# The first loads of an attention and gated-unit kernel: one hardware transfer instead of four, the rest cast on GpSimd's queue, and the first grams ahead of the transposes

## The chip, the cores and the metric

The kernel runs on one core of a Trainium2 chip. The metric is the device time of one execution in microseconds (us). "Before" and "after" are the kernel without and with the change. The medians of before in the four groups of experiments lie within 0.2 us (172.70 to 172.91), its single executions within 1.4 us (172.28 to 173.63), so a difference of 0.3 us between medians is near the limit of what can be told. Some changed kernels spread over 2 us; it is said where it matters. Ratios use runs in the fast state alone. Two runs, one of e8 and one of the repeat of e4, were in the slow state and are left out.

## The reference

Attention with pooled queries, then a gated unit with a causal convolution over time:

```python
q_pool = q.reshape(B, H, S // 2, 2, D).mean(axis=3)         # B = H = 8, S = 1152, D = 64
attn   = softmax(q_pool @ k.T / sqrt(D))
x      = (attn @ v), heads side by side                      # 8 x 576 x 512
gate   = sigmoid(causal convolution of x, 5 taps per channel)
out    = (gate * (x @ w_val)) @ w_out                        # float32
```

q, k and v are float32, 18.9 MB each. The kernel replaces the softmax by its first-order form (the scores are small; a flag computed at the end sends other data to an exact version). It therefore needs column sums of k and v and the "gram" matrices k-transposed times v, and uses q only after transposing it.

## The kernel before

Work goes by "slots" of four heads, sixteen slots in all. A slot has three loads (q, k, v), which GpSimd issues and which turn float32 into bfloat16 on the way. The first pair of heads was special: uncast loads through the hardware queues of SyncE and ScalarE, cast afterwards on VectorE and ScalarE.

```python
def load_slot(m, lo=0):                       # GpSimd's queue, with cast; lo: first head loaded
    ...
    nc.gpsimd.dma_start(out=qns[m][:, lo:], in_=q[...])
    for c, src in ((1, k), (0, v)):
        nc.gpsimd.dma_start(out=kvs[m][:, c, lo:], in_=src[...])

for h in range(2):
    nc.sync.dma_start(out=q0[:, h], in_=q[0, h]...)              # 2 x 0.29 MB, float32
nc.scalar.dma_start(out=kv0[:, 1], in_=k[0, 0:2]...)             # 0.59 MB
nc.sync.dma_start(out=kv0[:, 0], in_=v[0, 0:2]...)               # 0.59 MB
load_slot(0, 2)                               # second pair of slot 0: GpSimd, cast
...
warm(12)                                      # matmuls on zeros, for the clock
pool_q(0); transposes(0)
... wval, wout, load_slot(2), load_slot(3)
nc.vector.tensor_copy(out=kvs[0][:, 1, 0:2], in_=kv0[:, 1])      # cast of k
nc.scalar.copy(out=kvs[0][:, 0, 0:2], in_=kv0[:, 0])             # cast of v
pool_q(1)
# slot 0: sums(pair 0), grams(0), transposes(1), setup_conv, sums(pair 1), rows, grams(1), ...
# slot m: sums, rows, grams, ... ; load_slot(m + 4); output stores wait until all loads are issued
```

Of the kernel before, what the change touches and what calls it, by code (L numbers as in the profile page):

```python
# [7 lines left out]
FP32 = mybir.dt.float32  # L8
# [46 lines left out]
def first_order(ctx, tc, q, k, v, moe_w_val, moe_conv_w, moe_w_out, out, flag):  # L55
    nc = tc.nc
    B, H, S, D = q.shape
# [3 lines left out]
    NT = S // 128  # L61
# [4 lines left out]
    U = 6  # L66
    QP = Sq // U
# [9 lines left out]
    kv_pool = ctx.enter_context(tc.tile_pool(name="kvp", bufs=NKV))  # L77
    q_pool = ctx.enter_context(tc.tile_pool(name="qp", bufs=NKV))
# [12 lines left out]

    kvs, qns = {}, {}

    def load_slot(m, lo=0):
        b, h0 = divmod(4 * m, H)
        kvs[m] = kv_pool.tile([128, 2, 4, NT * D], BF16, name="kv", tag="kv")
        qns[m] = q_pool.tile([QP, 4, 2 * U * D], BF16, name="qn", tag="qn")
        nc.gpsimd.dma_start(out=qns[m][:, lo:], in_=q[b, h0 + lo:h0 + 4].rearrange("h (p s) d -> p h (s d)", p=QP))  # L98
        for c, src in ((1, k), (0, v)):
            nc.gpsimd.dma_start(out=kvs[m][:, c, lo:],  # L100
                                in_=src[b, h0 + lo:h0 + 4].rearrange("h (p t) d -> p h (t d)", p=128))


    q0 = q_pool.tile([QP, 2, 2 * U * D], FP32, name="q0", tag="qn")
    kv0 = kv_pool.tile([128, 2, 2, NT * D], FP32, name="kv0", tag="kv")
    for h in range(2):
        nc.sync.dma_start(out=q0[:, h], in_=q[0, h].rearrange("(p s) d -> p (s d)", p=QP))
    nc.scalar.dma_start(out=kv0[:, 1], in_=k[0, 0:2].rearrange("h (p t) d -> p h (t d)", p=128))
    nc.sync.dma_start(out=kv0[:, 0], in_=v[0, 0:2].rearrange("h (p t) d -> p h (t d)", p=128))

    wval_sb = consts.tile([128, NFT, Dm], BF16, name="wval_sb")
    wout_sb = consts.tile([128, NFT, Dm], BF16, name="wout_sb")
    convw_nat = consts.tile([KK, Dm], FP32, name="convw_nat")
    nc.sync.dma_start(out=convw_nat, in_=moe_conv_w)
    load_slot(0, 2)

    ident = consts.tile([128, 128], BF16, name="ident")
    nc.vector.memset(ident, 0.0)
# [17 lines left out]
    for i in range(2):  # L136
        for h in range(2):
            p = slice(64 * h + 32 * i, 64 * h + 32 * i + 32)
# [17 lines left out]
    for i in range(NX):  # L156
        t = xp_pool.tile([128, PAD + Sq], BF16, name=f"x{i}", tag=f"x{i}")
# [25 lines left out]
    for i in range(2):  # L183
        t = mq_pool.tile([128, 2, MQ], BF16, name=f"mq{i}", tag=f"mq{i}")
# [6 lines left out]

    def pool_q(n):
        m, i = divmod(n, 2)
        src = qns[m][:, 2 * i:2 * i + 2] if n else q0
        qv = src.rearrange("p h (u e d) -> p h u e d", u=U, e=2)
        qps[n] = work.tile([QP, U, 2, D], BF16, name="qp", tag="qp", bufs=3)
        nc.vector.tensor_tensor(out=qps[n].rearrange("p u h d -> p h u d"),  # L197
                                in0=qv[:, :, :, 0, :], in1=qv[:, :, :, 1, :], op=ALU.add)

    def transposes(n, at=None):  # L200
        m, i = divmod(n, 2)
        qp = qps.pop(n)
        qt_ps = (ps_t if at is None else ps_b).tile([128, Sq], BF16, name="qt_ps", tag="ts" if at is None else f"b{at}")
        qtv = qt_ps.rearrange("c (u p) -> c u p", u=U)
        for u in range(U):
            nc.tensor.transpose(out=qtv[:, u, :], in_=qp[:, u].rearrange("p h d -> p (h d)"),  # L206
                                identity=ident[0:QP, 0:QP])
        nc.scalar.copy(out=mq2[m % 2][:, i, 2 * D:].rearrange("c (p u) -> c p u", u=U),  # L208
                       in_=qt_ps.rearrange("c (u p) -> c p u", u=U))
# [15 lines left out]
    def grams(n):  # L225
        m, i = divmod(n, 2)
        kvv = kvs[m].rearrange("p c h (t d) -> p c h t d", t=NT)
        if i == 0:
            gs[m] = ps_g.tile([128, 512], FP32, name="g", tag="g")
        for t in range(NT):  # L230
            for h in range(2):
                nc.tensor.matmul(out=gs[m][64 * h:64 * h + 64, 128 * i:128 * i + 128].rearrange("p (c d) -> p c d", c=2),  # L232
                                 lhsT=kvv[:, 1, 2 * i + h, t, :], rhs=kvv[:, :, 2 * i + h, t, :],
                                 start=(i == 0 and t == 0), stop=(t == NT - 1), skip_group_check=True)
# [185 lines left out]
                             skip_group_check=True)  # L420

    warm(12)
    pool_q(0)
    transposes(0)
    nc.gpsimd.dma_start(out=wval_sb, in_=moe_w_val.rearrange("(ft p) n -> p ft n", p=128))
    nc.gpsimd.dma_start(out=wout_sb, in_=moe_w_out.rearrange("(ft p) n -> p ft n", p=128))
    load_slot(2)
    load_slot(3)
    nc.vector.tensor_copy(out=kvs[0][:, 1, 0:2], in_=kv0[:, 1])
    nc.scalar.copy(out=kvs[0][:, 0, 0:2], in_=kv0[:, 0])  # L430
    pool_q(1)
    for m in range(NSLOT):
        a, b = 2 * m, 2 * m + 1
        pb = b - 2
        odd = m % 2
        if m == 0:
            sums(m, (0,))
            grams(a)
            transposes(b, 1)
            setup_conv()  # L440
            sums(m, (1,))
            rows(m)
            grams(b)
        else:
            sums(m)
            rows(m)
            grams(a)
            grams(b)
        rank1(m)
        g = gs.pop(m)  # L450
        mevac(m, g)
        if not odd:

            bt = m // 2 - 1
            y, e = divmod(bt, 2)
            moe = bt >= 0
            if moe:
                pool_q(a + 2)
                tap(pb, 1)
            if moe:  # L460
                gval(bt, 2, val(bt, 2, 0))
            xhat(a, 1)
            xhat(b, 2)
            xevac(a)
            if moe:
                gate(pb)
            xevac(b)
            if m:
                norms(m - 1, g)
            squares_k(m, g)  # L470
            if moe:
                transposes(a + 2)
                gval(bt, 3, val(bt, 3, 0))
                stat(m - 1, g)
                pool_q(b + 2)
            else:
                pool_q(a + 2)
                transposes(a + 2)
            squares(m)
            conv(a, 1)  # L480
            conv(b, 2)
            tap(a, 0)
            if not moe:
                pool_q(b + 2)
            tap(a, 1)
            tap(a, 2)
            if moe:
                ops = big("ops", 0)
                outs(y, 512 * e, 4, ops, [0])
            transposes(b + 2)  # L490
            if moe:
                outs(y, 512 * e, 4, ops, [1])
                oevac(y, 512 * e, 4, ops)
            gate(a)
        else:

            bt = (m - 1) // 2
            y, e = divmod(bt - 1, 2)
            moe = bt > 0
            for i in range(3):  # L500
                tap(pb, i)
            if moe:
                if e:
                    ops = big("ops", 0)
                    outs(y, 1024, 1, ops, [0])
                    oevac(y, 1024, 1, ops)
                else:
                    ops = big("ops", 0)
                    outs(y, 0, 4, ops, [2])
            xhat(a, 1)  # L510
            xhat(b, 2)
            xevac(a)
            xevac(b)
            if moe and e:
                norms(m - 1, g)
            squares_k(m, g)
            if m + 1 < NSLOT:
                pool_q(a + 2)
                pool_q(b + 2)
            if moe:  # L520
                if e:
                    ops = big("ops", 0)
                    outs(y, 512, 4, ops, [2])
                    conv(a, 1)
                outs(y, 512 * e, 4, ops, [3])
                oevac(y, 512 * e, 4, ops, 2)
                if not e:
                    conv(a, 1, 1)
            else:
                conv(a, 1)  # L530
            if m + 1 == NSLOT:
                squares(m)
            conv(b, 2, 3 if m + 1 == NSLOT else 1)
            if not (moe and e):
                norms(m - 1, g)
            tap(a, 0)
            stat(m - 1, g)
            if m + 1 < NSLOT:
                transposes(a + 2)
            gate(pb)  # L540
            tap(a, 1)
            if e or not moe:
                tap(a, 2)
            if m + 1 == NSLOT:
                gate(b)
            else:
                tap(b, 0)
            gval(bt, 0, val(bt, 0, 1))
            if m < NSLOT - 1:
                transposes(b + 2)  # L550
            gate(a)
            gval(bt, 1, val(bt, 1, 0))
            if m + 1 < NSLOT:
                squares(m)
            if m == 1:
                warm(5, 1)
        if m + NKV < NSLOT:
            load_slot(m + NKV)
        else:
            while held:  # L560
                store(*held.pop(0), nc.gpsimd)
# [202 lines left out]
```

## Time and profile before

| | before |
|---|---|
| median | 172.77 us (172.68 to 173.12) |
| span in the profile | 170.5 us |
| matmul engine (PE) busy | 149.1 us, 87% |
| VectorE (DVE), ScalarE (ACT), GpSimd (POOL) busy | 125.1, 112.3, 44.1 us |
| HBM | 58.73 MB read, 9.44 MB written |

A busy share says how much an engine worked, not that the end waited for it. The prediction shows the rows that matter, those of the DMA rate and of the landings.

### The profile page before, as it was taken

The page shows a single profiled execution, that of the slowest core. Times are in us where ns is not written, and L with a number is a line of the kernel's source. Part 1 is how long each engine was busy: PE and PEld are TensorE (multiplying, and loading weights), DVE is VectorE, ACT ScalarE, POOL GpSimd, SP SyncE. Part 2 cuts the span into 40 slices and gives each one's busy share as a digit, 9 for nine tenths or more (in the row PEclk, how much of TensorE's full clock was granted, in tenths as well). Part 3 has the DMA queues.
Part 4 walks back from the last instruction along what each step waited for, and adds up shares of the span by engine and source line. Part 5 has one row for each costly group of instructions (what it writes and reads, how often), then busy time and mean ns, then how long its engine had stood idle before and what let it go on. Part 6 is the DMA issues. An engine that isn't in the chain of part 4 may idle for free.

```text
span 170.5 us, 4687 instructions
## 1 busy us (share of the span) xinstructions
PE 149.1 (87%) x1976; PEld 105.1 (62%) x1992; DVE 125.1 (73%) x245; ACT 112.3 (66%) x201; POOL 44.1 (26%) x70
## 2 busy tenths in 40 slices
PE   6439666779999999999999999999999999999930
PEld 2225444547676766876778668766876678668520
DVE  4315276956998699969996999599959996977520
ACT  3131586538777786978787769687868696877320
POOL 7963122312231313131223113131312121211000
PEclk9955599999999999999999999999999999999998
DMA  5999999999999999999999999999999999999993
GB/s 182 287 214 208 206 208 209 209 208 209 207 209 209 208 209 208 209 208 210 209 208 208 208 209 208 208 209 208 208 209 208 209 210 226 394 426 424 428 413 143
DMA packets 26131, 40.03 MB, mean 235 GB/s; under 512 B 1077, under 2 KB 23925, under 8 KB 25210
## 3 DMA queue, kind: packets, MB, share of 16 engines
q0 software_dynamic: 24896, 36.61, 107.6%
q1 hardware_dynamic: 794, 2.24, 3.9%
q10 hardware_dynamic: 416, 0.85, 1.4%
q8 instruction: 16, 0.26, 0.6%
q14 instruction: 9, 0.07, 0.1%
HBM read 58.73 MB, written 9.44 MB: 400 GB/s over the span
## 4 chain that ended last, share of the span: by engine, by line
PE 63%; DMA 18%; DVE 9%; ACT 3%; issue 2%; SPq 0%; DVEq 0%; ACTq 0%
PE ops L365 14%; PE vps L349 13%; DMA qn<-in_q_dram 13%; PE cps L311 9%; PE g L232 7%; DMA kv<-in_v_dram 5%; PE sm L222 5%; PE xh L287 4%; PE qt_ps L206 4%; PE ops L577 3%; PE g L249 2%; DVE acc L321 2%; PE g L260 2%; DVE rt L239 2%; DVE gv L357 1%
## 5 line engine op out<-in xcount | busy, mean ns | idle before, releaser
L326 DVE SCALAR_TENSOR_TENSOR acc<-x,convw_sb,acc 128x576 f32<-128x576 bf16 x51 | 41.6, 817 | 1.2
L349 PE MATMUL vps<-x,wval_sb 128*128 128x288 bf16 x256 | 36.6, 286 | 1.2 <-DVE acc L321 0.8
L357 DVE TENSOR_TENSOR gv<-vps,gate 128x576 bf16<-128x576 f32 x32 | 24.1, 754 | 12.0 <-PE vps L349 10.4
L365 PE MATMUL ops<-wout_sb,gv 128*128 128x512 bf16 x110 | 31.2, 380 | 0.7
L208 ACT COPY mq<-qt_ps 128x576 bf16<-128x576 bf16 x32 | 20.5, 640 | 16.1 <-PE qt_ps L206 15.8
L321 DVE SCALAR_TENSOR_TENSOR acc<-x,convw_sb,cps 128x576 f32<-128x576 bf16 x31 | 25.0, 808 | 6.1 <-PE cps L311 6.1
L294 ACT ACTIVATE x<-xh,vmean 128x576 bf16<-128x576 f32 x32 | 22.7, 738 | 8.2 <-PE xh L287 8.2
L349 PEld LDWEIGHTS <-wval_sb 128*128 128x128 bf16 x256 | 23.4, 97 | 7.1 <-issue 1.6
L333 ACT ACTIVATE gate<-acc 128x576 bf16<-128x576 f32 x31 | 21.2, 685 | 0.0
L311 PE MATMUL cps<-x,diag 128*128 128x288 bf16 x128 | 20.5, 293 | 0.7 <-ACT x L294 0.6
L232 PE MATMUL g<-kv 128*64 128x128 bf16 x576 | 20.3, 226 | 0.0
L98 POOL DMA_DIRECT2D qn<-in_q_dram x16 | 11.0, 686 | 35.8 <-DMA kv<-in_k_dram 20.0
L197 DVE TENSOR_TENSOR qp<-qn 96x768 bf16<-96x768 bf16 x31 | 16.5, 549 | 5.0 <-DMA qn<-in_q_dram 5.0
L232 PEld LDWEIGHTS <-kv 128*64 128x64 bf16 x576 | 17.4, 114 | 3.7 <-issue 3.7
L380 ACT COPY osb<-ops 128x1024 f32<-128x1024 f32 (+1 forms) x17 | 16.0, 940 | 5.3 <-PE ops L365 5.3
L279 ACT ACTIVATE sq<-mq 128x1152 bf16<-128x1152 bf16 x16 | 18.8, 1175 | 0.0
L100 POOL DMA_DIRECT2D kv<-in_k_dram x16 | 11.9, 745 | 26.6 <-PE qt_ps L206 7.8
L270 ACT ACTIVATE mq<-g 64x128 bf16<-64x128 f32 x32 | 8.7, 271 | 14.3 <-PE g L251 14.1
L100 POOL DMA_DIRECT2D kv<-in_v_dram x16 | 11.9, 742 | 23.9 <-DMA qn<-in_q_dram 21.4
L365 PEld LDWEIGHTS <-gv 128*128 128x128 bf16 x124 | 12.8, 112 | 7.7
L311 PEld LDWEIGHTS <-diag 128*128 128x128 bf16 x128 | 12.8, 100 | 6.7 <-issue 1.3
L206 PE MATMUL qt_ps<-ident,qp 96*128 96x96 bf16 x192 | 13.9, 210 | 2.6 <-DVE qp L197 2.6
(77 smaller groups left out, 148.6 us busy)
## 6 DMA issues: line engine op xcount, KB each, us to landing
qn<-in_q_dram POOLq DMA_DIRECT2D x15, 576.0 KB, 22.1
kv<-in_k_dram POOLq DMA_DIRECT2D x15, 576.0 KB, 22.1
kv<-in_v_dram POOLq DMA_DIRECT2D x15, 576.0 KB, 22.5
out_dram<-osb POOLq DMA_DIRECT2D x7, 1024.0 KB, 16.0
out_dram<-osb SPq DMA_DIRECT2D x2, 512.0 KB, 5.8
out_dram<-osb POOLq DMA_DIRECT2D x3, 256.0 KB, 16.4
kv<-in_k_dram ACTq DMA_DIRECT2D x1, 576.0 KB, 4.7
q<-in_q_dram SPq DMA_DIRECT2D x2, 288.0 KB, 4.2
```

What stands on the lines that cost most here:

```text
L100: nc.gpsimd.dma_start(out=kvs[m][:, c, lo:], in_=src[b, h0 + lo:h0 + 4].rearrange("h (p t) d -> p h (t d)", p=128))
L206: nc.tensor.transpose(out=qtv[:, u, :], in_=qp[:, u].rearrange("p h d -> p (h d)"), identity=ident[0:QP, 0:QP])
L208: nc.scalar.copy(out=mq2[m % 2][:, i, 2 * D:].rearrange("c (p u) -> c p u", u=U), in_=qt_ps.rearrange("c (u p) -> c p u", u=U))
L232: nc.tensor.matmul(out=gs[m][64 * h:64 * h + 64, 128 * i:128 * i + 128].rearrange("p (c d) -> p c d", c=2), lhsT=kvv[:, 1, 2 * i + h, t, : ...
L294: nc.scalar.activation(out=x[:, PAD:].rearrange("p (c n) -> p c n", c=2), in_=xhs.pop(n)[:, :, 0:HALF], func=AF.Identity, bias=vmean[:, m, ...
L311: nc.tensor.matmul(out=cps[:, half, 0:HALF], lhsT=w, rhs=x[:, c0:c0 + HALF], start=(i == 0), stop=(i == len(mats) - 1))
L321: nc.vector.scalar_tensor_tensor(out=acc.rearrange("p (c n) -> p c n", c=2), in0=x[:, kk:kk + Sq].rearrange("p (c n) -> p c n", c=2), scal ...
L326: nc.vector.scalar_tensor_tensor(out=accs[n], in0=x[:, kk:kk + Sq], scalar=convw_sb[:, ft, kk:kk + 1], in1=accs[n], op0=ALU.mult, op1=ALU.add)
L333: nc.scalar.activation(out=gt, in_=accs.pop(n), func=AF.Sigmoid)
L349: nc.tensor.matmul(out=vps[:, half, 0:HALF], lhsT=wval_sb[:, fi, ft * 128:(ft + 1) * 128], rhs=x[:, c0:c0 + HALF], start=(fi == 0), stop=( ...
L357: nc.vector.tensor_tensor(out=gvs[y, ft][:, e * Sq:(e + 1) * Sq].rearrange("p (c n) -> p c n", c=2), in0=vps[:, :, 0:HALF], in1=gates.pop( ...
L365: nc.tensor.matmul(out=ops[:, c % 2, :], lhsT=gvs[y, ft][:, t0 + c:t0 + 128 * m:m], rhs=wout_sb[:, ft, :], start=(ft == 0), stop=(ft == NF ...
```

## The change

The intent, as the diff shows it: fewer uncast bytes and casts in front of the first grams. Only k of the first pair comes through a hardware queue; v of slot 0 is loaded whole by GpSimd's queue, first in line, then q whole, then the rest of k. The first sums and grams no longer stand behind the transposes of q.

```diff
-    def load_slot(m, lo=0):
+    def load_slot(m):
...
+        def load(src, to, p, lo=0):
+            nc.gpsimd.dma_start(out=to[:, lo:], in_=src[b, h0 + lo:h0 + 4]...)
+        if m == 0:
+            load(v, kvs[m][:, 0], 128)
+        load(q, qns[m], QP)
+        load(k, kvs[m][:, 1], 128, 0 if m else 2)
+        if m:
+            load(v, kvs[m][:, 0], 128)
-    for h in range(2):
-        nc.sync.dma_start(out=q0[:, h], in_=q[0, h]...)
-    nc.scalar.dma_start(out=kv0[:, 1], in_=k[0, 0:2]...)
-    nc.sync.dma_start(out=kv0[:, 0], in_=v[0, 0:2]...)
+    nc.sync.dma_start(out=k0, in_=k[0, 0:2]...)
...
-    load_slot(0, 2)
+    load_slot(0)
...
     warm(12)
-    pool_q(0)
-    transposes(0)
...
-    nc.vector.tensor_copy(out=kvs[0][:, 1, 0:2], in_=kv0[:, 1])
-    nc.scalar.copy(out=kvs[0][:, 0, 0:2], in_=kv0[:, 0])
+    nc.vector.tensor_copy(out=kvs[0][:, 1, 0:2], in_=k0)
+    pool_q(0)
     pool_q(1)
...
             grams(a)
+            transposes(a, 0)
             transposes(b, 1)
```

More of the change, by code (lines that the diff above doesn't have):

```diff
@@ L97, in load_slot @@
         qns[m] = q_pool.tile([QP, 4, 2 * U * D], BF16, name="qn", tag="qn")
-        nc.gpsimd.dma_start(out=qns[m][:, lo:], in_=q[b, h0 + lo:h0 + 4].rearrange("h (p s) d -> p h (s d)", p=QP))
-        for c, src in ((1, k), (0, v)):
-            nc.gpsimd.dma_start(out=kvs[m][:, c, lo:],
-                                in_=src[b, h0 + lo:h0 + 4].rearrange("h (p t) d -> p h (t d)", p=128))
-    q0 = q_pool.tile([QP, 2, 2 * U * D], FP32, name="q0", tag="qn")
-    kv0 = kv_pool.tile([128, 2, 2, NT * D], FP32, name="kv0", tag="kv")
-    for h in range(2):
-        nc.sync.dma_start(out=q0[:, h], in_=q[0, h].rearrange("(p s) d -> p (s d)", p=QP))
-    nc.scalar.dma_start(out=kv0[:, 1], in_=k[0, 0:2].rearrange("h (p t) d -> p h (t d)", p=128))
-    nc.sync.dma_start(out=kv0[:, 0], in_=v[0, 0:2].rearrange("h (p t) d -> p h (t d)", p=128))
+        def load(src, to, p, lo=0):
+            nc.gpsimd.dma_start(out=to[:, lo:], in_=src[b, h0 + lo:h0 + 4].rearrange("h (p t) d -> p h (t d)", p=p))
+        if m == 0:
[4 more added lines that the diff above has]
+            load(v, kvs[m][:, 0], 128)
+    k0 = kv_pool.tile([128, 2, NT * D], FP32, name="k0", tag="kv")
+    nc.sync.dma_start(out=k0, in_=k[0, 0:2].rearrange("h (p t) d -> p h (t d)", p=128))
     wval_sb = consts.tile([128, NFT, Dm], BF16, name="wval_sb")
@@ L193, in pool_q @@
         m, i = divmod(n, 2)
-        src = qns[m][:, 2 * i:2 * i + 2] if n else q0
+        src = qns[m][:, 2 * i:2 * i + 2]
         qv = src.rearrange("p h (u e d) -> p h u e d", u=U, e=2)
```

## The prediction

> **What bounds the kernel now.** I began with the page's forty slices. The matmul engine (149.1 us busy of 170.5) looks like the bound, but the rows for the DMA are flatter than any row of an engine:
>
> ```profile
> PE   6439666779999999999999999999999999999930
> ...
> PEclk9955599999999999999999999999999999999998
> DMA  5999999999999999999999999999999999999993
> GB/s 182 287 214 208 206 208 209 209 208 209 207 209 209 208 209 208 209 208 210 209 208 208 208 209 208 208 209 208 208 209 208 209 210 226 394 426 424 428 413 143
> ...
> q0 software_dynamic: 24896, 36.61, 107.6%
> ...
> HBM read 58.73 MB, written 9.44 MB: 400 GB/s over the span
> ```
>
> The reader is to see that from the third slice (each 4.26 us) to the 33rd the rate stays at 206 to 214 GB/s, whether the matmul engine is a tenth idle or not. GB/s counts bytes written. The cast loads read float32 and write bfloat16, so 208.5 written is 417 GB/s read, about what the stores reach at the end (394 to 428). Reads of 58.73 MB at 417 take 140.8 us, stores of 9.44 MB at 425 take 22.2 us, together 163.0 us. One-microsecond windows show the engines at a share near 1 until 167 us and at 0.42 in 168 to 169. So 163 of 169 us are full transfer time, and only some 6 us can be won or lost by holes.
>
> Second, does compute follow the transfers? GpSimd keeps eight loads in flight; the order of its instructions shows that each issue waits for the load eight places earlier. GpSimd's timeline therefore dates landings. Two of the first slot's loads give the offset: issued at 2.13 and 2.85 us and landing 9.1 and 9.9 us later, at 11.23 and 12.75, they release issues at 11.54 and 13.02, so a landing is about 0.3 us before the issue that it releases:
>
> ```profile
> 11.54 0.74 POOL L100 DMA_DIRECT2D kv<-in_k_dram  x1 [0.99 <-DMA kv<-in_k_dram]
> 13.02 0.74 POOL L100 DMA_DIRECT2D kv<-in_v_dram  x1 [0.74 <-DMA kv<-in_v_dram]
> ...
> 21.47 0.74 POOL L100 DMA_DIRECT2D kv<-in_v_dram  x1 [1.77 <-DMA kv<-in_v_dram]
> ...
> 87.11 0.75 POOL L100 DMA_DIRECT2D kv<-in_k_dram  x1 [1.36 <-PE qt_ps L206]
> ...
> 95.61 0.74 POOL L100 DMA_DIRECT2D kv<-in_k_dram  x1 [2.12 <-PE qt_ps L206]
> ...
> 122.27 0.74 POOL L100 DMA_DIRECT2D kv<-in_k_dram  x1 [2.21 <-PE vps L349]
> ```
>
> These say that v of slots 1, 8, 9 and 12 landed by about 21.2, 86.8, 95.3 and 122.0 us. The matmul timeline has the column sums of the same slots, which need v, starting at 23.49, 87.66, 95.89 and 122.20. The early slot has 2.3 us of slack, the later ones 0.2 to 0.9. The chain of waits names mostly matmuls, since they take nearly as long per slot as the loads, but the loads set the pace. The chain's one long transfer, a load of q that lands at 124.5 us, says the same.
>
> Third, the start. The DMA view in windows, by queue (packets, MB, share of the engines), at 4.0 to 4.4, then 5.4 to 5.8, then 6 to 7 us:
>
> ```profile
> q10 hardware_dynamic: 71, 0.16, 109.4%
> ...
> q1 hardware_dynamic: 49, 0.08, 97.7%
> q0 software_dynamic: 3, 0.00, 6.3%
> ...
> q0 software_dynamic: 69, 0.11, 59.8%
> q1 hardware_dynamic: 72, 0.17, 47.6%
> ```
>
> q1 is SyncE's queue, q10 ScalarE's, q0 GpSimd's. The hardware queues move data from 1.6 us. GpSimd issues its first load at 1.35 us, and not a packet of it moves before 5.6, a full 4.2 us later; until then the hardware loads fill the engines alone. This is the fact on which I rest the prediction.
>
> **What the Trainium skill says.** *DMA: Bandwidth & Descriptors*, section *SWDGE vs HWDGE vs iDMA*, subsection *Issuing engines are not separate DMA queues*: transfers from any engine run on the same 16 DMA engines and interleave. The 6-to-7-us window agrees, both queues sharing them almost packet for packet. The same page's *Specifications* gives a first byte after about 0.6 us on the hardware path and about 1 us on GpSimd's. The trace has 0.85 us for SyncE (0.77 to 1.6) and 4.2 us for GpSimd's first, so the measurement decides and the page's 1 us is not used for it. *SBUF — State Buffer*, the box on the "DVE blocks DMA" trap, says that VectorE in a two-port mode keeps GpSimd from writing descriptors. VectorE is busy with memsets and a cast until 4.25 us, so this could be part of the 4.2 us, but the trace doesn't prove it. *TensorE: Matmul & The Clock Gate*, Part 1: the clock halves after an idle window of some 3.4 us. The clock row agrees: 0.5 from about 8.5 to 22 us, after the warm-up matmuls stop at 5.9.
>
> **The change part by part.**
> Removed: hardware loads of q (two, 288 KB each) and v (576 KB) and ScalarE's cast of v (1.15 us, just before the first sums at 11.14). q and v go instead to GpSimd's queue, as whole 576 KB loads cast on the way, v first; k of the first pair moves from ScalarE's queue to SyncE's. GpSimd's issues cost 0.68 to 0.78 us whatever the size, and their number, three for slot 0, is unchanged. The bytes read are unchanged too: 0.59 MB moves by hardware where 1.77 MB did, and 2.95 MB by GpSimd where 1.77 MB did. So the 140.8 us does not move; only holes do.
>
> The hole: k alone is 0.59 MB. In the first 1.4 us of flow before (1.6 to 3.0 us) 0.28 MB moved; the other 0.31 MB at 400 GB/s take 0.8 us. k is through near 3.9 us, and the engines then stand still until GpSimd's first packet, at a time S.
> Delivered by 10.0 us before: half-microsecond windows sum to 2.33 MB written; 1.78 MB of that came through hardware, so 0.55 MB was cast and counts twice, 2.89 MB read. After: 0.59 + 0.417 x (10.0 - S) MB.
> With S = 5.6 as before: 2.42 MB, 0.46 MB behind, or 1.1 us. With S = 5.0: 2.68 MB, 0.5 us. Break-even is S = 4.5. With S = 3.9 it is 0.6 us ahead, because the mixed phase of before (5.5 to 10 us, some 360 GB/s of reads) was itself not at full rate.
> I choose S = 5.2, deficit 0.29 MB, +0.7 us: part of the 4.2 us may be descriptor fetches behind saturated hardware queues, which now end sooner.
>
> The first slot's computation: v lands at S plus 2.83 us (1.18 MB at 417) plus about 1.2 us of completion lag (before, the last of slot 0 landed at 12.75 where its bytes alone give 11.6). With S = 5.2 that is 9.2 us, so sums and first grams start near 9.3 instead of 11.14. q lands 2.83 later, 12.0; pool additions (0.56 each) and twelve transposes (2 x 0.66 at half clock) bring the second sums to about 14.3, against 14.43. So the 1.9 us won by the first grams is lost again waiting for q. Even if some of it stayed, slot 1 has 2.3 us of slack and slot 2 is bounded by its landing, so it would not reach the end. The saved ScalarE cast and reordered VectorE work are off the path by the same reasoning.
> Sum: 172.77 + 0.7 = 173.5; I take 173.3, as the final drain (share 0.63 and 0.42 from 167 to 169 us) may hide part of a shift.
>
> **The rivals.**
> (1) Compute bounds it: the earlier grams carry through the chain of matmuls, and the end comes 1.5 to 2 us sooner, about 171. For: the chain is 63% matmul. Against: the flat rate, and slack below a microsecond at every late slot.
> (2) GpSimd's first packet comes about a microsecond after its issue ends, near 3.5 us: no hole, and less mixing, so about 172.2. For: the page's figure. Against: before, nothing moved on q0 at 4.0 to 4.4, when it should have been sharing.
> (3) Descriptor writing takes time per row, so that a first load of 512 rows instead of 192 starts later still: S = 6.5, +2.0 us, 174.8. For: the late start. Against: equal issue times for both sizes, and full rate ever after.
>
> **Range and chances.** S from 3.9 to 6.0 covers most of it: -0.6 to +1.3 us, widened by run-to-run spread (172.68 to 173.12). So 172.2 to 174.4. Two per cent is 3.5 us, more than half of all the holes there are: faster 0.02, slower 0.03, within 0.95.
>
> **What would show it.** Right: in the profile after, the DMA rate in the second or third half-microsecond from 4 us is near zero, q0's first packet is at 5 to 5.6 us, later slots are at 208 GB/s with their sums later by the same half to one microsecond, and the first sums start before 10 us. Wrong: q0 moving by 4 us, later landings earlier than before, or a matmul engine ahead of its loads by microseconds at slot 8.

## The result, and the profile after

After takes 174.58 us (174.35 to 174.85, six runs) where before took 172.89 in the same rounds: ratio 1.0096, interval 1.0080 to 1.0111. It is slower by 1.7 us, just outside the predicted range of 172.2 to 174.4. A ratio here is the mean time of one kernel's fast runs over that of the other's of the same rounds, so it is not quite the ratio of the medians that are quoted.

First the rows of the page of after that answer to those of before:

```profile
DMA  4999999999999999999999999999999999999992
GB/s 140 136 200 209 206 207 209 207 210 208 209 208 208 209 209 207 209 209 208 208 209 208 208 208 208 210 207 209 208 208 208 209 209 242 398 428 420 426 389 108
...
q0 software_dynamic: 25344, 37.20, 109.0%
...
HBM read 58.73 MB, written 9.44 MB: 395 GB/s over the span
```

The bytes are the same and the plateau is the same, 206 to 210 GB/s. Only the start differs. The digit rows hide it, as the DMA row shows 9 in both second slices, but the GB/s row says 136 where before had 287 (before's figure is partly uncast, so it is not comparable one to one).

The landings are next, from GpSimd's timeline of after (start, duration, instruction, and in brackets what ended the wait):

```profile
15.13 0.74 POOL L100 DMA_DIRECT2D kv<-in_v_dram  x1 [1.11 <-DMA kv<-in_k_dram]
...
23.21 0.74 POOL L100 DMA_DIRECT2D kv<-in_v_dram  x1 [1.88 <-DMA kv<-in_v_dram]
...
89.16 0.74 POOL L100 DMA_DIRECT2D kv<-in_k_dram  x1 [2.54 <-PE qt_ps L208]
...
123.92 0.75 POOL L100 DMA_DIRECT2D kv<-in_k_dram  x1 [2.19 <-PE vps L351]
```

The last three issues stood at 21.47, 87.11 and 122.27 us before, so these landings are later by 1.7 to 2.1 us. The first line, which waited for the last load of slot 0, stood at 13.02. The very last load lands 1.7 us later (148.89 against 147.22). The loss is complete early and is then carried to the end: summed from the packet records, after is behind before by 1.4 us worth of transfer at 12 us, and still by 1.4 at 20, 80 and 120 us.

So where do the first twenty microseconds lose it? The DMA view by queue in the windows of the prediction, 4.0 to 4.4, then 5.4 to 5.8, then 6 to 7 us:

```profile
q0 software_dynamic: 3, 0.00, 18.5%
...
q0 software_dynamic: 35, 0.04, 84.2%
...
q0 software_dynamic: 140, 0.16, 110.5%
```

GpSimd's queue (q0) is now alone. Three packets moved in the first window, 35 in the second and 140 in the third, where a microsecond of such packets at the plateau has about 180 (before, 15 to 16 us: 182). In half-microsecond windows, whose last columns are the granted clock, the DMA share and GB/s written, first after:

```profile
core 0: us, PE busy (x) PEld busy (x) DVE busy (x) ACT busy (x) POOL busy (x), PEclk, DMA share, GB/s
3.50:4.00 0.50, 0.50 (x3) 0.20 (x2) 0.00 (x0) 0.00 (x0) 0.44 (x3) 1.00 0.76 200
4.00:4.50 0.50, 0.50 (x3) 0.15 (x1) 0.48 (x2) 0.00 (x0) 0.50 (x1) 1.00 0.20 16
4.50:5.00 0.50, 0.50 (x2) 0.15 (x1) 0.50 (x1) 0.00 (x0) 0.50 (x2) 1.00 0.86 67
...
6.00:6.50 0.50, 0.50 (x2) 0.00 (x0) 0.00 (x0) 0.00 (x0) 0.50 (x3) 1.00 1.11 152
8.00:8.50 0.50, 0.00 (x0) 0.00 (x0) 0.00 (x0) 0.00 (x0) 0.50 (x2) 1.00 1.09 178
```

and the same places of before:

```profile
4.00:4.50 0.50, 0.50 (x3) 0.15 (x1) 0.23 (x1) 0.00 (x0) 0.50 (x1) 1.00 1.08 402
...
6.00:6.50 0.50, 0.00 (x0) 0.00 (x0) 0.00 (x0) 0.00 (x0) 0.45 (x4) 1.00 1.00 257
8.00:8.50 0.50, 0.00 (x0) 0.09 (x1) 0.18 (x1) 0.46 (x1) 0.50 (x2) 0.96 1.08 290
```

After has an almost empty half microsecond at 4.0 to 4.5 (16 GB/s), and then a long climb: 67, 85, 122, 152, 170, 168, 167, 178, 181 and only at 9.0 us 200 GB/s. The share at 4.5 to 5.0 is already 0.86 while the rate is a third of the plateau: the engines hold packets, but the packets last long. The single packet records say the same. The median packet of q0 takes 107 ns, as over the whole loading phase, but 36 of those that start between 3 and 9 us take over 200 ns, up to 1096 ns. Before has two such packets of q0 in the same time. I call these stalls.

The yardstick below is float32 bytes read: hardware bytes plus twice the bytes that q0 wrote. The DMA view from 0 to 12 us, first after, then before (packets, MB, share):

```profile
q0 software_dynamic: 994, 1.26, 69.9%
q1 hardware_dynamic: 282, 0.60, 14.8%
...
q0 software_dynamic: 801, 0.96, 46.1%
q1 hardware_dynamic: 506, 1.19, 33.2%
q10 hardware_dynamic: 272, 0.59, 13.3%
```

That is 3.12 MB after and 3.70 MB before. The difference of 0.58 MB at 417 GB/s is 1.4 us, most of the loss.

The start of the matmul chain of after shows what the first part of the intent brought:

```profile
9.92 1.15 PE L224 MATMUL sm<-kv,first 128*32 128x512 bf16 x6 [3.37 <-DMA kv<-in_v_dram]
10.99 1.17 PE L234 MATMUL g<-kv 128*64 128x128 bf16 x18
13.63 1.14 PE L208 MATMUL qt_ps<-ident,qp 96*128 96x96 bf16 x12 [1.46 <-DVE qp L199]
...
15.22 1.15 PE L224 MATMUL sm<-kv,first 128*32 128x512 bf16 x6
```

The first sums start 1.2 us earlier than before (9.92 against 11.14), the second sums 0.8 us later (15.22 against 14.43), as q is now late.

### The profile page after: what moved, and what is told of

It is laid out like the page before. It is cut to its first block, busy times and chain, and to the rows that moved or that the text cites. A ratio compares the mean times of both kernels' runs of the same rounds, so it can differ in the third digit from the quotient of the medians.

```text
span 172.7 us, 4696 instructions
## 1 busy us (share of the span) xinstructions
PE 153.2 (89%) x1992; PEld 106.7 (62%) x1992; DVE 124.7 (72%) x245; ACT 111.1 (64%) x200; POOL 43.1 (25%) x70
## 4 chain that ended last, share of the span: by engine, by line
PE 67%; DMA 23%; DVE 3%; ACT 1%; issue 1%; DVEq 0%; ACTq 0%; POOLq 0%
PE vps L351 18%; PE ops L367 16%; DMA qn<-in_q_dram 12%; PE cps L313 9%; PE g L234 8%; DMA out_dram<-osb 6%; DMA kv<-in_v_dram 5%; PE sm L224 5%; PE qt_ps L208 4%; PE xh L289 4%; PE g L251 2%; PE g L262 2%; DVE gv L359 1%; ACT x L296 1%; DVE rt L241 1%
## 5 line engine op out<-in xcount | busy, mean ns | idle before, releaser
L351 PE MATMUL vps<-x,wval_sb 128*128 128x288 bf16 x256 | 38.5, 295 | 0.9 <-DVE acc L323 0.5
L367 PE MATMUL ops<-wout_sb,gv 128*128 128x512 bf16 x124 | 31.9, 380 | 0.0
L351 PEld LDWEIGHTS <-wval_sb 128*128 128x128 bf16 x256 | 24.1, 100 | 7.4 <-issue 1.1
L208 PE MATMUL qt_ps<-ident,qp 96*128 96x96 bf16 x192 | 14.5, 217 | 2.0 <-DVE qp L199 2.0
```

What stands on the lines that cost most here:

```text
L208: nc.tensor.transpose(out=qtv[:, u, :], in_=qp[:, u].rearrange("p h d -> p (h d)"), identity=ident[0:QP, 0:QP])
L351: nc.tensor.matmul(out=vps[:, half, 0:HALF], lhsT=wval_sb[:, fi, ft * 128:(ft + 1) * 128], rhs=x[:, c0:c0 + HALF], start=(fi == 0), stop=( ...
L367: nc.tensor.matmul(out=ops[:, c % 2, :], lhsT=gvs[y, ft][:, t0 + c:t0 + 128 * m:m], rhs=wout_sb[:, ft, :], start=(ft == 0), stop=(ft == NF ...
```

## The experiments

Sixteen runs of fifteen kernels were made (e4 ran twice), in four groups; each group shared its chip and its runs of before, whose medians were 172.83, 172.91, 172.71 and 172.70 us. After itself was not run again beside them, so each kernel is best compared by its ratio to before, where after has 1.0096. All results were correct. "MB by 12" is the yardstick just explained, in the profiled run. Several expectations speak of theory A: the loss lies in the transfers of the first microseconds, not in the computation.

### Which half of the change costs

**Order alone (e1).** Transfers of before, order of work of after.

```diff
-    pool_q(0)
-    transposes(0)
...
+    pool_q(0)
     pool_q(1)
...
             grams(a)
+            transposes(a, 0)
             transposes(b, 1)
```

> Transfers of before, order of work of after (first grams, then both pairs of transposes). Theory A (the 1.7 us come from a stretch near 4 to 9 us in which GpSimd's queue delivers little, so from the transfers): within 0.3 us of before, 172.6 to 173.2. Rival B (the first slot's computation, 0.8 us later in the changed kernel at the second sums, carries to the end): at least half of the loss, 173.7 or more.

Measured: 172.66 us, ratio 0.9994 (0.9979 to 1.0009), 3.68 MB by 12. The new order by itself costs nothing and brings nothing.

**Transfers alone (e2).** The reverse: after with the q addition and transposes of the first pair again ahead of the sums.

> Transfers of after, order of work of before (transposes of the first pair, which need q, ahead of the first grams). Theory A: the same as after within 0.3 us, 174.3 to 174.9, although the grams now wait for q at 12.7 us. Rival B: grams 3 us later, so slower than after by a microsecond or more, 175.6 and up.

Measured: 175.04 us, ratio 1.0121 (1.0101 to 1.0141), 3.30 MB by 12. The loss comes with the transfers alone, as theory A says, but the kernel is 0.4 us slower than after, beyond the 0.3 I allowed, though its loads were not behind after's (3.30 against 3.12 MB). The end shows why. Windows of this kernel from 164 us:

```profile
164.00:165.00 1.00, 1.00 (x8) 0.31 (x7) 0.00 (x0) 0.99 (x3) 0.00 (x0) 1.00 0.66 279
165.00:166.00 1.00, 1.00 (x7) 0.52 (x7) 0.83 (x5) 0.35 (x1) 0.00 (x0) 1.00 0.69 287
166.00:167.00 1.00, 0.88 (x9) 0.54 (x6) 0.10 (x2) 0.86 (x2) 0.00 (x0) 1.00 0.92 381
```

In after the share is 0.97, 0.93 and 1.00 in these three. Here the sums of slot 0 started at 15.13 us, the matmul engine was still 1.5 to 2 us behind after's from slot 2 on, and SyncE issued its last two stores at 164.78 instead of 163.23 us. The transfers ran dry at 164 to 166 us waiting for output. There are thus two bounds at the end, the drain of the transfers and the last stores, and a late matmul engine reaches the time only where it opens such holes.

### How many bytes through the hardware queues

**k and v (e3).** After, with v of the first pair uncast on ScalarE's queue: 1.18 MB by hardware (after 0.59, before 1.77).

```diff
+    nc.scalar.dma_start(out=kv0[:, 0], in_=v[0, 0:2]...)
...
-            load(v, kvs[m][:, 0], 128)
+            load(v, kvs[m][:, 0], 128, 2)
...
+    nc.scalar.copy(out=kvs[0][:, 0, 0:2], in_=kv0[:, 0])
```

> After, with v of the first pair also uncast through a hardware queue (ScalarE's): 1.18 MB by hardware, where after has 0.59 and before 1.77. Theory A: the second 0.59 MB fills engines that were starved, 0.59/0.417 = 1.4 us at most, less what GpSimd's queue moved there: 173.2 to 173.8, sums of slots 4 to 12 about 1 us earlier than in after. Rival B: sums start on v at about 6 us but q bounds the first slot as before: 174.3 or more.

Measured: 172.81 us, ratio 1.0004 (0.9988 to 1.0019), 3.83 MB by 12, v of slot 2 landing by 35.9 us against 37.9. This second 0.59 MB wins back the whole 1.7 us, a little more than I had allowed. GpSimd's queue begins at 5.3 us and is at 205 GB/s as soon as it is alone.

The kernel has a surprise for theory B (computation sets the time). Its sums of slot 1 are the earliest of all (23.14 us), yet those of slot 2 come 2.1 us later than before (38.13 against 36.08), and all later ones stay 1.3 to 2 us late, at no cost. Matmul timelines, e3 first:

```profile
30.62 0.43 PE L210 MATMUL qt_ps<-ident,qp 96*128 96x96 bf16 x6 [1.47 <-DVE qp L201]
31.82 2.08 PE L353 MATMUL vps<-x,wval_sb 128*128 128x288 bf16 x8 [0.76 <-DVE acc L325]
```

then before:

```profile
30.51 0.43 PE L206 MATMUL qt_ps<-ident,qp 96*128 96x96 bf16 x6 [0.21 <-DVE qp L197]
31.70 1.15 PE L349 MATMUL vps<-x,wval_sb 128*128 128x288 bf16 x8 [0.76 <-DVE acc L321]
```

Both need q of slot 2, which lands at 29.9 us in before and 30.0 in e3. The kernel that was ahead waits 1.5 us for it, its granted clock falls to half at 31.0 us, and its next eight matmuls take 2.08 us instead of 1.15. A lead in computation was turned into a lag by the wait for the next load.

**Nothing by hardware (e4, and again as a repeat).** After without any hardware load of q, k or v.

> After, with nothing through the hardware queues: k of slot 0 whole on GpSimd's queue. Theory A: if GpSimd's first packet stays at 3.6 us with the same slow climb, the 0.59 MB that k moved before 3.8 us come on top, +1.4 us on after: 175.6 to 176.3. If the start of GpSimd's queue is held back by the hardware traffic itself (in before it began at 5.6, when 1.77 MB ran ahead of it), it starts nearer 2.5 us and the loss is half a microsecond or none: 174.3 to 175.2. Rival B: 174.6 plus up to 1 us, as k then lands later.

Measured: 174.25 us, ratio 1.0093 (1.0047 to 1.0138), 3.43 MB by 12. The time is in the range of the second reading, and GpSimd's first packet came at 2.9 us, so hardware traffic in front of it does hold its start back. But the queue was near its full rate from 4.0 us (180, then 207 GB/s): a slow climb of five microseconds is not how this queue must begin. The six times spread from 173.26 to 175.65, so it ran again.

> The kernel with nothing through the hardware queues a second time, as its six times spread from 173.3 to 175.7 while its one profile showed stalls only until 4.2 us. If the spread is that of the stalls, a profile at another time shows another length of slow climb: at 175 or more, 2.3 MB or less read by 10 us; at 173.5 or less, 2.6 MB or more.

Measured: 174.30 us, 17 fast runs from 173.06 to 175.56, ratio 1.0100 (1.0076 to 1.0124). The profiled run was the quickest, 173.06 us, with 3.47 MB by 12; the earlier profile, at 174.37 us, had 3.43. In both nearly all stalls end by about 4.1 us, so between these two the spread is not that of the stalls, and my reading was wrong. The profiles differ at the end: the slower one issues its last two stores at 164.07 instead of 162.36 us and has holes at 164 and 166 us (shares 0.78 and 0.72). That is the second bound again. No profile caught the runs at 175.4 to 175.7. Of the 24 runs of this kernel, the eight up there have mean granted clocks of 0.909 to 0.919, all others 0.928 or more, which fits a late matmul engine and the second bound, but is not shown.

**A useless load (e6).** After, with 0.59 MB that nobody reads on ScalarE's queue.

```diff
+    fill = consts.tile([128, 2, NT * D], FP32, name="fill")
+    nc.scalar.dma_start(out=fill, in_=v[B - 1, H - 2:H]...)
```

> After, with a useless 0.59 MB load (the last pair of v, uncast, never read) on ScalarE's hardware queue beside k. It adds 0.59/0.417 = 1.4 us of transfer. Theory A (hardware bytes fill time in which GpSimd's queue delivers little anyway, as with v in the k-and-v run): the extra bytes cost nothing or almost nothing, 174.0 to 175.0. Rival (GpSimd's queue loses a fixed time whenever it starts): 1.4 us slower than after, 175.8 to 176.3.

Measured: 173.88 us, ratio 1.0054 (1.0041 to 1.0067). Each measured against its own before, it is 0.7 us faster than after although it moves 0.59 MB, or 1.4 us, more; even theory A had expected no gain. Windows of this kernel:

```profile
4.00:4.50 0.50, 0.50 (x3) 0.15 (x1) 0.23 (x1) 0.00 (x0) 0.50 (x1) 1.00 1.04 410
...
6.00:6.50 0.50, 0.50 (x2) 0.00 (x0) 0.50 (x1) 0.00 (x0) 0.50 (x2) 1.00 1.23 212
8.00:8.50 0.50, 0.00 (x0) 0.00 (x0) 0.00 (x0) 0.00 (x0) 0.50 (x2) 1.00 1.21 207
```

There is no hole and no climb, 207 to 212 GB/s at once, and no packet of q0 over 200 ns. This is the clearest experiment. The transfers of after lose at least as much time to hole and stalls as 0.59 MB of traffic costs, and traffic in front of GpSimd's queue removes both. With that traffic the queue also starts later (first packet at 5.3 us); e11 below delays it without.

**Everything by hardware (e8).** All 3.54 MB of slot 0 uncast through the two hardware queues, cast on VectorE and ScalarE.

> The opposite of the change: all of slot 0 (3.54 MB) uncast through the two hardware queues, cast on VectorE and ScalarE; GpSimd's queue begins with slot 1. Theory A: the engines are fed at 400 GB/s through the whole start, 2.9 to 3.2 MB read by 10 us against 2.88 in before, so equal to before or up to 0.7 us faster, 172.1 to 172.9. Rival B (compute of the first slot): with all casts on the engines, slower than before by 0.5 us or more.

Measured: 175.55 us, the median of three fast runs (a fourth, at 178.35, was slow), ratio 1.0146 (1.0125 to 1.0168). Theory A's figure missed. The hardware queues run at 400 GB/s only until GpSimd's queue joins at 5.9 us; then the three share the engines, 3.52 MB are read by 12 us (before 3.70), and the second pair arrives last, so the second sums start at 19.76 us. At the end the shares at 164, 165 and 167 us are 0.62, 0.46 and 0.51: the second bound. More hardware bytes are not simply better.

### What the stalls are not

**The cast on VectorE (e5).** After casts k on VectorE at 4.24 us, in the middle of the climb.

```diff
-    nc.vector.tensor_copy(out=kvs[0][:, 1, 0:2], in_=k0)
+    nc.scalar.copy(out=kvs[0][:, 1, 0:2], in_=k0)
```

(The cast of the float32 identity was moved behind the q additions too.)

> After, with the cast of k (0.94 us on VectorE at 4.24 us) moved to ScalarE and the cast of the float32 identity behind the q additions, so that VectorE is idle from 3.4 us until q lands. Theory C (VectorE's cast keeps GpSimd from writing descriptors): total written in 4.5 to 6.0 us rises from 67 to 122 towards 200 GB/s, 2.6 MB or more read by 10 us instead of 2.32, and the time falls by 0.5 to 1.0 us, 173.6 to 174.1. Theory D (the stall is in the queue itself, whatever VectorE does): the same slow climb and 174.3 to 174.9. The transfers-only run, whose VectorE was idle then and which still climbed slowly, speaks for D.

Measured: 174.58 us, ratio 1.0082 (1.0062 to 1.0103), 3.20 MB by 12, with 92, 115, 88 and 120 GB/s in the four windows from 4.5 us. The stalls are still there, while VectorE does nothing from 3.3 to 13.4 us, so theory C falls. (The profiled run is the slowest of six that spread from 173.91 to 175.54 us; it has holes at 164 and 166 us too, shares 0.77 and 0.75.)

**The order of q and v (e9).** The two swapped on GpSimd's queue.

> After, with q ahead of v on GpSimd's queue. Theory D2 (the slow climb is a limit of rows per microsecond, as rows of q are 1536 bytes and rows of v 1152): a third more bytes in 4.5 to 6 us, loads 0.3 us earlier. Theory A without it: loads land at the same times as in after, but v and so the first sums come at about 12.7 instead of 9.9 us. If only the loads set the end, 174.3 to 174.9; if the matmul chain, late by 2 us, becomes the bound as in the transfers-only run (last stores issued at 164.8 instead of 163.2, holes at 163 to 168 us), 174.8 to 175.4.

Measured: 174.97 us, ratio 1.0118 (1.0100 to 1.0135), 3.04 MB by 12, with 86, 65 and 111 GB/s from 4.5 us. Rows a third longer do not help, so a limit in rows per microsecond is not it. First sums at 13.14 us, 3.2 later than in after, cost 0.4 us at most.

**Slot 1's issues (e7).** After, with GpSimd issuing slot 1's loads at 9.48 us instead of 3.90, behind four memsets of 128x1024 float32.

> After, with GpSimd issuing slot 1's three loads (3.9 to 6.2 us in after) only when its memsets and some 3 us of extra memset work are done, so that it writes no new descriptors while the engines work through slot 0's. Theory S1 (packets stall because the queue is being filled while it is drained): the packets of 300 to 1100 ns go, 167 GB/s or more at 4.5 to 6 us, 0.7 to 1.2 us faster than after, 173.4 to 173.9. Theory S2 (the queue stalls early for another reason): same slow climb, 174.3 to 175.0.

Measured: 175.05 us, ratio 1.0133 (1.0105 to 1.0161). The stalls of the first microseconds stayed (134, 138 and 161 GB/s from 4.5 us), so filling the queue while it is drained is not the cause. New ones came at 11 to 16 us, when slot 1's descriptors were used within 2 to 6 us of their issue (155 to 170 GB/s at 12 to 14 us).

### When GpSimd's queue starts

**1.4 us later (e11).** After, with two such memsets in front of GpSimd's first issue, which comes at 2.67 instead of 1.30 us.

> After, with GpSimd's first issue held back by about 1.5 to 2 us of memset work: its queue starts later, but with no hardware traffic in front of it. If a late start in itself cures the stalls (as the filler's run could also be read), the queue climbs at once to 200 GB/s from about 5.5 us and the time is 174.3 to 174.9, the hole paid for by the cure. If the hardware traffic or the lead of descriptors written meanwhile is what cures them, the stalls stay and the shift comes on top: 175.5 to 176.5.

Measured: 173.27 us, ratio 1.0042 (1.0028 to 1.0057), 3.50 MB by 12. It loses 0.6 to 0.7 us (by medians, by the ratio) where after loses 1.7, and is a microsecond better than the better reading. Windows of this kernel:

```profile
4.00:4.50 0.50, 0.50 (x3) 0.15 (x1) 0.00 (x0) 0.00 (x0) 0.50 (x2) 1.00 1.06 39
...
5.00:5.50 0.50, 0.50 (x2) 0.15 (x1) 0.13 (x1) 0.00 (x0) 0.48 (x2) 1.00 0.95 127
6.00:6.50 0.50, 0.33 (x2) 0.00 (x0) 0.27 (x1) 0.00 (x0) 0.50 (x1) 1.00 1.17 198
```

The hole is wider than in after (39 and 35 GB/s from 4.0 to 5.0 us) and the queue stalls at first, but only for a microsecond: 22 of its 24 packets over 200 ns start between 4.2 and 5.3 us, and from 5.5 us the rate is full (205, 198, 217). The 0.2 MB by which it is behind before at 10 us, 0.5 us, is nearly all of its loss.

**One memset (e14), one head (e15), two queues (e12), the other queue (e13).** These four are after with one memset in front of GpSimd's first issue, meant to delay it by 1 us; with one head of k by hardware instead of two; with one head each on SyncE's and ScalarE's queue; and with both on ScalarE's.

> After, with GpSimd's first issue 1 us late instead of the 2 us that cured the stalls. k ends near 3.8 us; GpSimd's first packet came 1.3 to 2.3 us after its issue, here 3.6 to 4.6. Theory T: if it starts after k has ended, stalls only for about a microsecond and 173.0 to 173.5, faster than with 2 us since the hole is 1 us shorter or absent; if it meets k's last packets again, 174.3 or more.

> After, with only one head of k (0.29 MB) through the hardware queue, three through GpSimd's. The hardware traffic ends near 3.0 us. Theory T: GpSimd's queue starts at 2.6 to 3.6 us, at or after that end: stalls either short, with 2.6 MB read by 10 us and 173.4 to 174.2, or as in after where the two meet. As the second head of k comes last, the first sums start at 12.5 to 13 us, which the q-first run suggests costs 0 to 0.4 us.

> After, with k's two heads on SyncE's and ScalarE's hardware queues, one each, the same 0.59 MB. All five kernels so far with k alone on SyncE's queue and GpSimd issuing at 1.3 us have shown packets of 300 to 1100 ns until 9 us or later; the kernels with two hardware queues have not. Theory Q (one queue or two decides): no such packets, 2.65 MB or more read by 10 us, 173.2 to 173.8. Theory T (the moment decides: GpSimd's queue starts just as the hardware traffic ends): stalls as in after, 174.3 to 175.

> After, with k on ScalarE's hardware queue instead of SyncE's. Theory T and theory Q (one queue): stalls as in after, 174.3 to 175.0. If something of SyncE's queue itself mattered: no stalls, 173.2 to 173.8.

| | median us | ratio (95% interval) | profiled run: us, MB by 12, packets of q0 over 200 ns until 10 us |
|---|---|---|---|
| before | 172.70 | | 172.58, 3.70, 2 |
| e14 | 173.25 | 1.0019 (1.0002 to 1.0037) | 173.37, 3.56, 29 |
| e15 | 173.84 | 1.0081 (1.0050 to 1.0113) | 173.39, 3.59, 35 |
| e12 | 173.21 | 1.0026 (1.0009 to 1.0043) | 173.44, 3.58, 43 |
| e13 | 174.61 | 1.0087 (1.0064 to 1.0110) | 172.88, 3.66, 39 |
| after | 174.58 | 1.0096 (1.0080 to 1.0111) | 174.75, 3.12, 40 |

(The rows of before and after give their first profiles; after's median and ratio are of its own rounds, and it was not run beside these four.) Neither of my two rules holds. In e14 and e12 GpSimd's queue did meet the last packets of k (3.5 to 4.0 us), as in after, and yet they lost a fifth to a third as much: "the moment decides" falls. The delay in e14 failed, too: most of the memset fell into time in which GpSimd had waited anyway, so the first issue came only 0.36 us later (1.66 us) and the first packet no later (3.59 us, 3.62 in after). That e14 gains is thus not explained by a later start. e12 had two queues and still stalled: "one queue or two" falls in its strict form.

e13 had four runs at 174.0 to 174.8, like after, and one at 172.88, which is the one that was profiled, and whose loads were hardly behind; whether its other runs stalled longer was not profiled. e15 falls into two clusters, seven runs at 173.4 to 174.0 us and four at 175.0 to 175.5, again those with the lowest clock (0.910 or 0.911 against 0.932 or more); its profile is of the quicker cluster, and its first sums waited for k until 13.31 us, where 12.5 to 13 was expected. Counting long packets does not rank these kernels. The bytes by 12 us do roughly, within this table: e8 with 3.52 MB took 176.16 us and the repeat of e4 with 3.47 took 173.06, as e8's profile has the holes at the end and the other has not.

### A version to beat both

**e3 with idle matmuls in the wait (e10).** Seven matmuls on zeros in slot 1 keep the clock up in e3.

```diff
+            if m == 1:
+                warm(7, 0)
             if m + 1 < NSLOT:
                 transposes(a + 2)
```

> The k-and-v kernel with seven idle matmuls in slot 1 while the matmul engine waits for q of slot 2 (28.8 to 30.6 us), to keep its clock up. There the loads ran 0.1 to 0.3 us ahead of before, but the matmuls of 31 to 38 us at half clock left the sums of slot 2 two microseconds late and holes at 163 and 165 us. With the clock kept: sums of slot 2 near 36.0, no holes at the end, 172.4 to 172.8, at best 0.2 per cent faster than before. If lateness of the matmul engine costs nothing, 172.8 as without.

Measured: 172.84 us, ratio 1.0005 (0.9989 to 1.0021). The mechanism worked, as this kernel's matmul timeline shows (1.15 us for the eight matmuls that took 2.08 in e3):

```profile
31.15 1.15 PE L353 MATMUL vps<-x,wval_sb 128*128 128x288 bf16 x8 [0.16 <-DVE acc L325]
```

Sums of slot 2 start at 35.42 us, 2.7 earlier than in e3, and the last stores go out at 160.99 instead of 162.91. The time did not move. The profiled run, at 173.62 us one of the slower of 14, shows that the issue of the last stores is not the bound here: its last two hardware stores are issued 0.6 us before those of before (162.87 and 163.64 us) and land later (170.22 and 170.46 against 168.95 and 169.58). What held them is not shown. No kernel tried is faster than before beyond its interval.

## Why the prediction was wrong

**What bounds the kernel** was read rightly. Every kernel with later loads was slower; in e1, e3 and e10 the matmul engine is up to 2 us later or 0.6 us earlier than before, at equal time. The second bound, the last stores behind a late matmul engine, was not in the prediction; it cost e2 another 0.4 us.

**Slips in readings and sums.** I gave 23.49 us as the start of slot 1's sums, which is their weight load. The matmuls start at 24.29, so the slack was 3.1 us, not 2.3. The first data packet of a hardware queue starts at 1.79 us, not 1.6, so SyncE's delay was 1.0 us, not 0.85. The clock row agrees with a window of 3.4 us only in its length: the full clock lasts from 5.05 to 8.46 us, though matmuls run for 1.3 us of that. And S = 6.0 in the formula gives 2.26 MB, a loss of 1.5 us and not 1.3; the range would then have reached about 174.6. That would have covered the time without mending the step that failed.

**The hole.** "k is through near 3.9 us, and the engines then stand still" is what happened: k's last data moved at 3.8 us and 16 GB/s flowed at 4.0 to 4.5. That GpSimd's queue would start sooner with less hardware traffic in front was right too, and more so than I chose: first packet at 3.6 us, not 5.2. The prediction had listed "q0 moving by 4 us" as a sign that it was wrong, and it was one.

**The step that failed** is the formula "After: 0.59 + 0.417 x (10.0 - S) MB", in which the queue runs at full rate from its first packet. By 10 us 2.32 MB had been read, which is the formula's answer for S = 5.85, although the first packet came at 3.6. The difference of 2.2 us is the stalls, a term that the sum did not have. With the true S of 3.6 the formula would have given 3.26 MB, a gain of 0.9 us. That the sign of the prediction was right is therefore luck: a start put too late stood in for part of the stalls. e11 tests the rest of the formula: a queue that is at full rate from 5.5 us has read 2.67 MB by 10 us, the formula's answer for S = 5.0, and loses 0.6 to 0.7 us where the formula has 0.5.

**From MB to time.** The deficit by 12 us is 1.4 us, the last load lands 1.7 us late and the time is 1.7 us longer. Where the last 0.3 us comes from is not shown. (One difference in the traces: in after, rows of v and of q, 1152 and 1536 bytes, are mixed from 7 to 9.5 us; before changes from q to k within 1.5 us.)

**The first slot.** I had first sums near 9.3 us and second sums at 14.3; they came at 9.92 and 15.22. That the gain of the first grams is lost again waiting for q, and would not reach the end if kept, was right (e1, e9).

**The rivals.** (1) falls: the earlier grams brought nothing. (2) had the start of the queue right, 3.6 us, and its consequence wrong. (3) came nearest in time, 174.8, for a reason that the trace refutes: the first load of 512 rows did not start later, and row length did not matter (e9).

**Range.** The range allowed for uncertainty in when the queue starts, none for how it runs once started.

**Open.** What makes the packets stall. Shown is that hardware traffic of 1.2 MB or more in front removes it, useful or not (e3, e6, e10), that a first issue 1.4 us later shortens it to a microsecond (e11), and that the cast, the order of q and v, and slot 1's issues are not it. Nor is it one queue or two, or the meeting with k's last packets, by themselves. Untested are a difference between chips, as after itself was not run again beside the experiments, and which of the 16 engines a long packet ran on, which the kept traces do not tell.

## What to carry to other kernels

Where transfers bound a kernel, look first at what a change to its first microseconds does to the bytes moved by then, not at what it does to the first computation: add up what each queue has delivered by a fixed time and compare. Then look at the end for holes, since a late matmul engine can add to the loss (e2). In this kernel 1.2 to 1.8 MB through the hardware queues in front of GpSimd's cast loads were worth keeping even though they need a cast on an engine, since they fill the time in which GpSimd's queue starts; 3.5 MB were too much (e8). An engine that is made early only to wait for the next load can come out late, by its clock.

## What the Trainium skill lacked or had wrong

- *DMA: Bandwidth & Descriptors*, section *Specifications*: its first byte of about 1 us for GpSimd's path is too short here and no constant. From the start of the first issue to the first packet it was 1.6 us with no hardware load of q, k or v in front (e4), 2.3 us behind 0.59 MB, 4.0 us behind 1.18 MB (e3) and 4.3 us behind 1.77 MB.
- No page of the skill has that GpSimd's queue, alone just after a hardware load, may have packets of 200 to 1100 ns and run at 67 to 181 GB/s for 4.5 us where its plateau is 208, nor that a useless 0.59 MB hardware load in front made the kernel 0.7 us faster.
- *SBUF — State Buffer*, the box on the "DVE blocks DMA" trap: its one cause for a GpSimd-issued load that seems held up is VectorE. It is not the cause of these stalls: with VectorE idle they stayed (88 to 120 GB/s at 4.5 to 6.5 us in e5, 174.58 us as before the move). The box itself is not refuted by that.
